# Sliding-window attention and a gated MLP in one kernel: the early heads kept apart by partitions, their copies merged, the planner's constants replaced

## The chip, the core and the metric

The program runs on one NeuronCore of a Trainium2 chip. The metric is the device time of one execution in microseconds (us). TensorE is called PE here, ScalarE ACT, VectorE DVE, GpSimd POOL, and the queue that issues nearly all DMAs is SP. TensorE's clock has two levels, 1.2 and 2.4 GHz; the granted share of the higher one stands in the rows (1.00 is 2.4 GHz).

## What is computed

```python
# q, k, v: (4 batches, 8 heads, 768 positions, 64), float32; n_sink = 4, window = 128
scores = q @ k.transpose(0, 1, 3, 2) / sqrt(64)
keep = (pos_k < n_sink) | ((pos_q - pos_k >= 0) & (pos_q - pos_k < window))
a = softmax(where(keep, scores, -1e9))
x = (a @ v).transpose(0, 2, 1, 3).reshape(3072, 512)
h = x @ w_in              # w_in: 512 x 2048, float64
out = (h * cos(h)) @ w_out  # w_out: 2048 x 512, float64
```

The weights arrive as float64 and are turned into float32 on the chip by integer operations. Products are made either in plain float32 (two records of a matmul in the trace, with two passes over the moving operand each) or in float32r (one pass), with each operand split into a high part and a rest and three float32r matmuls in place of one.

## The kernel before

The 3072 positions are cut into 12 chunks of 256 (`NT`): chunk 0, 1 and 2 are the first 256 positions of the batches 0, 1 and 2, and the others follow. For each chunk the attention of 8 heads gives x transposed (128 partitions for two heads, so four pairs), split into `xhi` and `xlo`; then eight dense slots each compute 256 columns of h (24 matmuls of `h_mm`, line 482), gate them on ACT and DVE, and multiply them into two accumulators of 128 rows (`out_mm`, lines 537 to 542). Chunk 0's `out_mm` runs in plain float32 (line 537), the others in three float32r matmuls (line 542).

The heads of chunks 0 to 2 are the early heads (`NEH` = 24, that is 12 pairs). They see 256 queries and 256 keys, and they stay in plain float32. One pair goes as follows.

- Two DMAs each load q and k of both heads side by side (128 columns, 64 for each head). `pe_turn` (line 887) turns q and then k on PE into the two halves of one PSUM tile `qk` in bank b3.
- `q_out` copies the q half to `tq`. `k_out` copies the k half twice, 64 partitions each, into `kz`: head 0 in partitions 0 to 63 of its first half, head 1 in partitions 64 to 127 of its second half, zeros elsewhere (a memset in `setup`, line 298). These copies are lines 470 on ACT and 472 on DVE, whichever the planner picks.
- `scores_pe` (line 912) makes one matmul for each of the two query blocks j over all 128 partitions; the zeros keep the heads apart. Its moving operand has 2x128 columns for j = 0 and 2x256 for j = 1. Bank "s" holds the scores; in chunk 0, j = 1 uses bank b1.
- `mask` (DVE, line 981), `expo` (ACT, line 990), `denom` and `norm` (lines 1004 to 1015) make the softmax.
- For each head `turn` (line 1087) transposes the three blocks of probabilities, `p_out` copies them to SBUF into the single tile `firsts[:, 0]`, and `values_pe` (line 1139) multiplies them with V. V of both heads is the 128-column stationary operand, so the result of a head has 128 rows of which 64 are of use; the two heads lie side by side in one bank.
- `x_hi` (line 410) is one ACT copy of 64 partitions for each head, `x_minus` (line 417) subtracts it on PE with one 512-column matmul, and `x_lo` is one copy of 64 partitions for each head.

A planner orders all of this before the kernel is written out: every step has a due time made from the constants in `C`, a list of engines with estimated durations, and the steps it waits for. The order on each engine is then fixed, and PE runs its instructions in that order. Until the first matmul of line 537, `fill` (line 1444) puts 256-column dummy matmuls where the plan shows PE idle. The 32 pieces of the weights (512 KB each) are decoded on DVE in three operations each (lines 603, 609, 615) and split on ACT and DVE (lines 642, 645) during the same stretch.

Of the kernel before, what the change touches and what calls it, by code (L numbers as in the profile page):

```python
# [16 lines left out]
P = 128  # L17
# [11 lines left out]
    "AE": 2.711, "ALT": 0.594, "CK": 62.564, "DA": -4.325, "DH": -1.102, "DM": 2.191, "DQ": 2.945, "DS": 4.986,  # L29
    "DV": 3.356, "DX": 0.796, "E": [-3.526, -24.976, 17.898], "GAP": 0.45, "GHI": 2, "GLO": 2, "L": 1, "LAG": 3.882,  # L30
    "LB": 14.146, "LEAD": 15.611, "LP": -23.228, "NE": -17.921, "NEH": 24, "NM": -6.28, "PASS": 2, "PB": 5, "PEN":
    2.331, "PL": 3, "POOLF": 1.446, "POOLPEN": 1.649, "QE": 8.731, "R": 2, "RAW": 3, "S0": -8.701, "S1": 54.633,
    "SE": 2.011, "SO": 5.722, "SO2": -10.441, "STEP": 7.518, "T": 7.132, "TE": [-9.794, -13.102, 9.173], "TQ":
    4.529, "VE": 31.258, "WARM": 4, "WI": -10.037, "WO": 10.858, "WS": 0.701, "WS2": 1.922, "WT": 2, "XE": 5.901,
    "XV": 2,
# [197 lines left out]
def attn_moe_kernel(ctx, tc, q, k, v, n_sink, window, w_in, w_out, out):  # L233
# [56 lines left out]
    def setup():  # L290
# [7 lines left out]
        nc.gpsimd.memset(env.kz, 0.0)  # L298
# [95 lines left out]
    def new_chunk():  # L394
        x = Rec()
        x.acc, x.o, x.f, x.bo = {}, {}, {}, {}
        x.sums = [[] for _ in range(NP)]
        x.parts, x.full, x.om = [], False, {}
        x.last = False
        return x  # L400

    def x_hi(x, a, p, odd):
        def fn(e):
            if p == 0 and not odd:
                x.hi = xp.tile([P, NP, NT], F32R, name=f"xhi_{a}", tag="xhi", bufs=2)
            if odd is None:
                nc.scalar.copy(out=x.hi[:, p, :], in_=x.f[p])
            else:
                r = slice(odd * 64, odd * 64 + 64)
                nc.scalar.copy(out=x.hi[r, p, :], in_=x.f[p][r, odd])  # L410
        return fn

    def x_minus(x, p):
        def fn(e):


            nc.tensor.matmul(
                out=x.f[p], lhsT=minus, rhs=x.hi[:, p, :].unsqueeze(1).broadcast_to([P, 2, NT]),
                start=False, stop=True, skip_group_check=True,
            )  # L420
        return fn

    def x_lo(x, a, p, odd):
        def fn(e):
            if p == 0 and not odd:
                x.lo = xp.tile([P, NP, NT], F32R, name=f"xlo_{a}", tag="xlo", bufs=2)
            if odd is None:
                e.tensor_tensor(out=x.lo[:, p, :], in0=x.f[p], in1=f32(x.hi)[:, p, :], op=ALU.subtract)
            else:
                r = slice(odd * 64, odd * 64 + 64)  # L430
                copy(e, x.lo[r, p, :], x.f[p][r, odd])
        return fn

    def split_x(plan, x, a, p, t, odd=None):

        add, buf = plan.add, plan.buf
        if p == 0 and not odd:
            x.bhi, x.blo = buf("xhi", 2), buf("xlo", 2)
        i = add(
            [("ACT", act(NT, odd is None))], x_hi(x, a, p, odd), x.sums[p] + (x.firsts[:1] if x.parts else [x.bhi]), t, skew=odd == 1  # L440
        )
        if odd == 0:
            x.head, x.first_hi = i, x.parts == []
            if x.first_hi:
                x.firsts, x.parts = [i], [[]]
            else:
                x.parts.append([])
            return [i]
        users = [i]
        if odd is None:  # L450
            j = add(sub(NT), x_lo(x, a, p, odd), [i, x.firsts[1] if x.parts else x.blo], t + 0.3, port=True, lock=True)
            if not x.parts:
                x.firsts = [i, j]
            x.parts.append([i, j])
            return users + [j]
        m = add([("PE", 0.34)], x_minus(x, p), [x.head, i], t + 0.3)
        users.append(m)
        env.minus.users.append(m)
        for half in range(2):
            d = [m] + x.firsts[1:2] if x.firsts[1:] else [m, x.blo]  # L460
            j = add([("ACT", act(NT, False)), ("DVE", dve(NT))], x_lo(x, a, p, half), d, t + 0.6 + 0.01 * half, skew=half == 1)
            if not x.firsts[1:]:
                x.firsts.append(j)
            users.append(j)
        x.parts[p] += [x.head] + users
# [272 lines left out]
    def banded_path():  # L738
# [11 lines left out]
        env.kz = firsts[:, 1].rearrange("p (a n) -> p a n", a=2)  # L750
# [131 lines left out]
        def pe_turn(o, part, tile, n):  # L882
            def fn(e):
                if part == 0:
                    o.qk = ps.tile([P, 2, NT], F32, name=f"qk_{o.tag}", tag="b3")
# [7 lines left out]
        def q_out(o):  # L893
            def fn(e):
                o.tq = ap.tile([P, NT], F32, name=f"tq_{o.tag}", tag="tq")
                copy(e, o.tq, o.qk[:, 0])
            return fn

        def k_out(o, odd):
            def fn(e):  # L900
                r = slice(odd * 64, odd * 64 + 64)
                copy(e, env.kz[r, odd, : o.nkb * P], o.qk[r, 1, : o.nkb * P])
            return fn

        def scores_pe(o, o1, j):
            def fn(e):
                i, w = o.i0 + j, o.w[j]
                pool = env.pa if o.s_banks[j] in ACC else ps
                s_ps = pool.tile([P, 2, NT], F32, name=f"s_{o.tag}_{j}", tag=o.s_banks[j])
                o.s_ps[j], o1.s_ps[j] = s_ps[:, 0], s_ps[:, 1]  # L910
                c0 = max(i - 1 - o.kb0, 0) * P
                nc.tensor.matmul(  # L912
# [754 lines left out]
```

## Time and profile before

| | us |
|---|---|
| median of 3 runs (lowest, highest) | 725.0 (724.86, 725.3) |
| the profiled execution | 725.11 |
| its span, first to last instruction | 723.4 |
| PE, DVE, ACT, POOL busy in it | 711.6, 624.4, 551.7, 104.4 |

Busy time is summed over instructions without overlap. A matmul's end is modelled: it covers the way through the array, so consecutive matmuls overlap in the rows, and what one costs is the step from its start to the next start. A row with "x4" merges four records. The mean granted clock was 0.997.

### The profile page before, as it was taken

The page shows a single profiled execution, that of the slowest core. Times are in us where ns is not written, and L with a number is a line of the kernel's source. Part 1 is how long each engine was busy: PE and PEld are TensorE (multiplying, and loading weights), DVE is VectorE, ACT ScalarE, POOL GpSimd, SP SyncE. Part 2 cuts the span into 40 slices and gives each one's busy share as a digit, 9 for nine tenths or more (in the row PEclk, how much of TensorE's full clock was granted, in tenths as well). Part 3 has the DMA queues.
Part 4 walks back from the last instruction along what each step waited for, and adds up shares of the span by engine and source line. Part 5 has one row for each costly group of instructions (what it writes and reads, how often), then busy time and mean ns, then how long its engine had stood idle before and what let it go on. Part 6 is the DMA issues. An engine that isn't in the chain of part 4 may idle for free.

```text
span 723.4 us, 14936 instructions
## 1 busy us (share of the span) xinstructions
PE 711.6 (98%) x4746; PEld 634.3 (88%) x4746; DVE 624.4 (86%) x1803; ACT 551.7 (76%) x1373; POOL 104.4 (14%) x180
## 2 busy tenths in 40 slices
PE   8999999999999999999999999999999999999996
PEld 6787776999999999999999999999899999999995
DVE  6999999788998999999999999887889998865432
ACT  4989958486978978879879789779788798784431
POOL 1000100002121121121221211322010122212000
PEclk9999999999999999999999999999999999999998
DMA  5886673132852764565465333323232332100001
GB/s 158 225 229 182 209 203 79 34 58 41 208 141 42 175 148 103 140 166 111 109 180 144 83 74 62 71 40 52 49 83 42 68 65 47 33 27 7 31 0 34
DMA packets 215895, 71.47 MB, mean 99 GB/s; under 512 B 204288, under 2 KB 204800, under 8 KB 215808
## 3 DMA queue, kind: packets, MB, share of 16 engines
q1 hardware_dynamic: 215232, 70.17, 40.4%
q8 instruction: 40, 0.66, 0.4%
q14 instruction: 47, 0.39, 0.2%
q10 hardware_dynamic: 576, 0.26, 0.1%
HBM read 64.10 MB, written 6.29 MB: 97 GB/s over the span
## 4 chain that ended last, share of the span: by engine, by line
PE 91%; ACT 4%; DVE 4%; issue 1%; POOL 0%; POOLq 0%; ACTq 0%; DVEq 0%
PE h L482 37%; PE acc L542 33%; PE av L1163 6%; PE s L968 5%; PE acc L537 4%; PE tp L1083 2%; PE av L1139 1%; PE s L912 1%; ACT p L990 1%; PE tp L1087 1%; DVE p L981 1%; ACT firsts L470 1%; PE gp L1067 0%; PE qk L887 0%; DVE p L1015 0%
## 5 line engine op out<-in xcount | busy, mean ns | idle before, releaser
L482 PE MATMUL h<-xhi,lo_in 128*128 128x256 f32 x768 | 226.6, 295 | 0.0
L482 PE MATMUL h<-xlo,hi_in 128*128 128x256 f32 x768 | 217.0, 283 | 0.0
L482 PE MATMUL h<-xhi,hi_in 128*128 128x256 f32 x768 | 216.7, 282 | 0.0
L482 PEld LDWEIGHTS h<-xhi,lo_in 128*128 128x128 f32 x768 | 146.0, 190 | 5.9 <-issue 1.4
L482 PEld LDWEIGHTS h<-xhi,hi_in 128*128 128x128 f32 x768 | 146.2, 190 | 4.4 <-issue 2.1
L482 PEld LDWEIGHTS h<-xlo,hi_in 128*128 128x128 f32 x768 | 146.0, 190 | 0.0
L542 PE MATMUL acc<-hi_out,ghi 128*128 128x512 f32 x350 | 141.4, 404 | 0.0
L542 PE MATMUL acc<-hi_out,glo 128*128 128x512 f32 x350 | 137.4, 393 | 0.0
L542 PE MATMUL acc<-lo_out,ghi 128*128 128x512 f32 x350 | 137.3, 392 | 0.0
L1122 POOL TENSOR_SCALAR_AFFINE_SELECT pz<-pz 128x512 fp32r<-128x512 f32 x128 | 84.8, 662 | 269.6 <-DVE pz L1109 204.5
L990 ACT ACTIVATE p<-p,st 128x264 f32<-128x264 f32 (+1 forms) x192 | 93.2, 488 | 0.3
L491 ACT ACTIVATE yt<-h 128x512 int32<-128x512 f32 x96 | 57.0, 594 | 45.0 <-PE h L482 43.7
L504 ACT ACTIVATE r<-r,neg 128x512 f32<-128x512 f32 x96 | 69.4, 724 | 26.7 <-DVE r L497 26.1
L981 DVE CUSTOM_DVE_ANT_0 p<-s,mk 128x264 f32<-128x264 f32 (+1 forms) x192 | 75.2, 398 | 16.7 <-PE s L968 11.9
L497 DVE SCALAR_TENSOR_TENSOR r<-h,yt 128x512 f32<-128x512 f32 x96 | 65.5, 682 | 23.3 <-ACT yt L491 22.9
L542 PEld LDWEIGHTS acc<-hi_out,glo 128*128 128x128 f32 x350 | 65.8, 188 | 14.8
L509 DVE TENSOR_TENSOR h<-h,r 128x512 f32<-128x512 f32 x88 | 60.8, 691 | 14.3 <-ACT r L504 14.2
L542 PEld LDWEIGHTS acc<-hi_out,ghi 128*128 128x128 f32 x350 | 66.0, 189 | 8.1
L542 PEld LDWEIGHTS acc<-lo_out,ghi 128*128 128x128 f32 x350 | 66.2, 189 | 7.7
L527 DVE TENSOR_TENSOR glo<-h,ghi 128x512 fp32r<-128x512 f32 x88 | 60.1, 684 | 10.4 <-ACT ghi L521 9.9
L521 ACT CAST ghi<-h 128x512 fp32r<-128x512 f32 x88 | 51.5, 585 | 21.0 <-PE acc L542 13.0
L968 PE MATMUL s<-r,l 128*128 128x264 f32 (+2 forms) x288 | 59.6, 288 | 0.0
(139 smaller groups left out, 1262.0 us busy)
## 6 DMA issues: line engine op xcount, KB each, us to landing
raw<-in_moe_w_in_dram SPq DMA_DIRECT2D x32, 512.0 KB
raw<-in_moe_w_out_dram SPq DMA_DIRECT2D x32, 512.0 KB
xk<-in_k_dram SPq DMA_DIRECT2D x256, 48.0 KB
v<-in_v_dram SPq DMA_DIRECT2D x64, 96.0 KB
out_dram<-raw SPq DMA_DIRECT2D x22, 256.0 KB
xq<-in_q_dram SPq DMA_DIRECT2D x144, 32.0 KB
v<-in_v_dram SPq DMA_DIRECT2D x32, 64.0 KB
xq<-in_q_dram SPq DMA_DIRECT2D x24, 64.0 KB
```

The lines of the kernel that those rows point to most:

```text
L482: nc.tensor.matmul(out=o.h[:, t, :], lhsT=w[:, fs], rhs=xx[:, c, :], start=(c == 0 and n == 0), stop=(c == NC - 1 and n == 2),)
L491: nc.scalar.activation(out=yt, in_=o.h, func=AF.Copy, scale=INV2PI, bias=0.25)
L497: nc.vector.scalar_tensor_tensor(out=o.r, in0=o.h, scalar=INV2PI, in1=yt, op0=ALU.mult, op1=ALU.subtract)
L504: nc.scalar.activation(out=o.r, in_=o.r, func=AF.Sin, scale=TWOPI_DOWN, bias=quarter)
L509: nc.vector.tensor_tensor(out=o.h, in0=o.h, in1=o.r, op=ALU.mult)
L521: nc.scalar.copy(out=o.ghi, in_=o.h)
L527: e.tensor_tensor(out=o.glo, in0=o.h, in1=f32(o.ghi), op=ALU.subtract)
L542: nc.tensor.matmul(out=x.acc[j], lhsT=gg[:, t, j * P : (j + 1) * P], rhs=w, start=(f == 0 and n == 0), stop=(f == NFT - 1 and n == 2), ski ...
L968: nc.tensor.matmul(out=o.s_ps[j][:, :w], lhsT=o.l[:, j * P : (j + 1) * P], rhs=r.rearrange("p n s -> p (n s)")[:, c0 : c0 + w], start=(n = ...
L981: nc.vector.tensor_tensor_reduce(out=o.p[:, j, :w], in0=o.s_ps[j][:, :w], in1=masks[min(o.i0 + j, 2)][:, :w], op0=ALU.add, op1=ALU.min, sc ...
L990: nc.scalar.activation(out=o.p[:, j, :w], in_=o.p[:, j, :w], func=AF.Exp, bias=o.lead.st[:, 0, o.nth, j : j + 1], scale=-1.0, accum_out=o. ...
L1122: nc.gpsimd.affine_select(out=env.pz4[:, :, :, n], in_=f32(env.pz4)[:, :, :, 0], pattern=[[0, 2], [0, CB], [sign, P]], compare_op=ALU.is_g ...
```

## The change

For the early heads only:

- q and k are copied together, in one copy of 512 columns, from PSUM to a plain tile `qks`. There is no `kz` with zeros.
- The scores of the two heads are separate matmuls, each on 64 partitions (0 to 63 or 64 to 127 of both operands): four of them in one step, 128 columns each for j = 0 and 256 for j = 1. The first head's scores go to bank "s", the second head's into the bank in which q and k were turned. In chunk 0 that bank alternates between b3 and b1, in chunks 1 and 2 it is b3.
- `p_out` has one buffer for each head of a pair.
- `values_pe` uses the 64 columns of V of its own head and writes to the 64 partitions of that head, so a pair's result is one 128x256 tile.
- `x_hi`, `x_minus` and `x_lo` are done once for a pair, on 128 partitions and 256 columns.
- The planner's constants are other numbers. The later heads and the dense part keep their operations.

```diff
 C = {
-    "AE": 2.711, ... "E": [-3.526, -24.976, 17.898], ... "S1": 54.633, ... "T": 7.132, ...
+    "AE": 17.984, ... "E": [-46.005, -27.161, 3.366], ... "QK": 1, ... "S1": 51.346, ... "T": 8.536, ...
...
-        nc.gpsimd.memset(env.kz, 0.0)
...
-            i = add([("ACT", act(NT, odd is None))], x_hi(x, a, p, odd), ..., skew=odd == 1)
-        m = add([("PE", 0.34)], x_minus(x, p), [x.head, i], t + 0.3)
-        for half in range(2):
-            j = add([("ACT", act(NT, False)), ("DVE", dve(NT))], x_lo(x, a, p, half), d, ...)
+        i = add([("ACT", act(NT, not packed))], x_hi(x, a, p), x.sums[p] + (x.firsts[:1] or [x.bhi]), t)
+            d = [add([("PE", 0.125)], x_minus(x, p), [i], t + 0.3)]
+        on = [("ACT", act(NT, False)), ("DVE", dve(NT))] if packed else sub(NT)
+        j = add(on, x_lo(x, a, p, packed), d + (x.firsts[1:] or [x.blo]), t + 0.6, ...)
...
-                copy(e, o.tq, o.qk[:, 0])
-                copy(e, env.kz[r, odd, : o.nkb * P], o.qk[r, 1, : o.nkb * P])
+                o.qks = ap.tile([P, 2, NT], F32, name=f"qks_{o.tag}", tag="qks", bufs=C["QK"])
+                copy(e, o.qks, o.qk)
...
-                    out=s_ps[:, :, :w], lhsT=o.tq[:, j * P : (j + 1) * P], rhs=env.kz[:, :, c0 : c0 + w],
+                sa = ps.tile([P, 2, NT], F32, name=f"s_{o.tag}", tag="s")
+                for j in range(CB):
+                    c0 = max(o.i0 + j - 1 - o.kb0, 0) * P
+                    for n, (oo, s_ps) in enumerate(((o, sa), (o1, o.qk))):
+                        oo.s_ps[j] = s_ps[:, j]
+                        r = slice(n * D, (n + 1) * D)
+                        nc.tensor.matmul(
+                            out=s_ps[:, j, : o.w[j]], lhsT=o.qks[r, 0, j * P : (j + 1) * P],
+                            rhs=o.qks[r, 1, c0 : c0 + o.w[j]], start=True, stop=True,
+                        )
...
-                o.pt = firsts[:, 0]
+                o.pt = firsts[:, o.odd]
...
-                    x.f[o.pair] = ps.tile([P, 2, NT], F32, name=f"av_{o.tag}", tag=o.av_bank)
+                    x.f[o.pair] = ps.tile([P, NT], F32, name=f"av_{o.tag}", tag=o.av_bank)
+                r = slice(o.odd * D, (o.odd + 1) * D)
-                    dst = x.f[o.pair][:, o.odd, (qs[0] - o.i0) * P : (qs[-1] + 1 - o.i0) * P]
-                    mms.append((dst, o.v2[:, kb - o.kb0], o.pt[:, o.offs[n] * P : o.offs[n + 1] * P]))
+                    dst = x.f[o.pair][r, (qs[0] - o.i0) * P : (qs[-1] + 1 - o.i0) * P]
+                    mms.append((dst, o.v2[:, kb - o.kb0, r], o.pt[:, o.offs[n] * P : o.offs[n + 1] * P]))
...
-            o.s_banks, o.tp_bank, o.av_bank = ("s", "s"), "tp", "av"
+            o.qk_bank, o.tp_bank, o.av_bank = "b3", "tp", "av"
             if o.a == 0:
-                o.s_banks, o.tp_bank, o.av_bank = ("s", "b1"), ("tp", "b4")[o.odd], ("av", "b2")[o.pair % 2]
+                o.qk_bank, o.tp_bank, o.av_bank = ("b3", "b1")[o.pair % 2], ("tp", "b4")[o.odd], ("av", "b2")[o.pair % 2]
...
-                pt, bpt = buf(o.tp_bank, 1), buf("phi", 1)
+                pt, bpt = buf(o.tp_bank, 1), buf(("phi", "plo")[o.odd], 1)
...
+                        o.sc = add([("PE", 4 * 2 * sum(o.w) / 2400)], scores_pe(o, heads[g + 1]), [*o.kr, bs], ...)
+                        o.bqk.users.append(o.sc)
+                        o.bs, heads[g + 1].bs = bs, o.bb
...
-                x.bav.users += split_x(plan, x, o.a, o.pair, t + DA + 5.0, o.odd)
+                if o.odd:
+                    x.bav.users += split_x(plan, x, o.a, o.pair, t + DA + 5.0, True)
```

## Rows read from the trace of the kernel before

**Rows 1.** The page: busy time of each engine and the chain that ended last.

```profile
PE 711.6 (98%) x4746; PEld 634.3 (88%) x4746; DVE 624.4 (86%) x1803; ACT 551.7 (76%) x1373; POOL 104.4 (14%) x180
...
PE 91%; ACT 4%; DVE 4%; issue 1%; POOL 0%; POOLq 0%; ACTq 0%; DVEq 0%
```

**Rows 2.** Windows: length; busy us (records) of PE, PEld, DVE, ACT, POOL; clock; DMA.

```profile
0.00:20.00 20.00, 17.68 (x93) 13.94 (x93) 13.11 (x68) 10.23 (x32) 2.86 (x11) 1.00 0.60 157
20.00:42.75 22.75, 20.33 (x118) 15.55 (x117) 22.36 (x74) 21.87 (x71) 0.00 (x0) 1.00 0.86 233
42.75:57.90 15.15, 15.15 (x111) 13.71 (x110) 14.79 (x40) 12.58 (x31) 0.00 (x0) 1.00 0.69 211
57.90:125.70 67.80, 67.47 (x348) 47.43 (x347) 66.81 (x162) 54.43 (x132) 3.05 (x4) 1.00 0.61 170
```

**Rows 3.** Groups: xcount | busy us, mean ns | idle before; dummies.

```profile
L1444 PE MATMUL idle<-gt 128*128 128x256 f32 x79 | 13.4, 315 | 0.1
```

**Rows 4.** PE in order of time: start, duration, what; idle before, releaser.

```profile
35.75 2.64 PE L1444 MATMUL idle<-gt 128*128 128x256 f32 x20
...
39.29 0.82 PE L1139 MATMUL av<-firsts,v 128*128 128x256 f32 x4
...
41.54 0.92 PE L1139 MATMUL av<-firsts,v 128*128 128x256 f32 x4 [0.98 <-ACT xhi L410]
...
42.75 0.68 PE L482 MATMUL h<-xhi,lo_in 128*128 128x256 f32 x1
...
45.31 0.36 PE L482 MATMUL h<-xhi,lo_in 128*128 128x256 f32 x1
```

**Rows 5.** PE in order of time, steps from start to start.

```profile
43.86 0.39 PE L417 MATMUL av<-xhi,gt 128*128 128x512 f32 x1
44.10 0.49 PE L1087 MATMUL tp<-ident,p 128*128 128x128 f32 x3
...
49.03 0.28 PE L482 MATMUL h<-xhi,hi_in 128*128 128x256 f32 x1
49.15 0.28 PE L482 MATMUL h<-xlo,hi_in 128*128 128x256 f32 x1
...
52.04 1.02 PE L912 MATMUL s<-firsts,tq 128*128 128x512 f32 x2
...
53.13 0.49 PE L1087 MATMUL tp<-ident,p 128*128 128x128 f32 x3
```

**Rows 6.** Windows of line 417 alone: PE and PEld; after the first dense matmul.

```profile
42.75:125.70 82.95, 4.79 (x8) 1.50 (x8) 1.00 0.63 177
125.70:723.40 597.70, 0.75 (x2) 0.19 (x1) 1.00 0.36 81
```

**Rows 7.** Groups again: ACT copies that the change merges, one of 512 columns.

```profile
L491 ACT ACTIVATE yt<-h 128x512 int32<-128x512 f32 x96 | 57.0, 594 | 45.0 <-PE h L482 43.7 <-DVE gc L1053 0.6
...
L410 ACT CAST xhi<-av 64x256 fp32r<-64x256 f32 x24 | 8.8, 366 | 2.7 <-PE av L1139 1.4 <-PE h L482 1.0
...
L470 ACT COPY firsts<-qk 64x256 f32<-64x256 f32 x20 | 7.3, 366 | 5.0 <-PE qk L887 4.6
...
L470 ACT CAST xlo<-av 64x256 fp32r<-64x256 f32 x17 | 6.2, 365 | 0.2
```

**Rows 8.** Windows of line 912 alone (scores), after the first dense matmul.

```profile
42.75:125.70 82.95, 8.96 (x22) 3.02 (x20) 1.00 0.63 177
```

**Rows 9.** PE in time: a later head's values, weights 128 and 64 wide.

```profile
426.26 0.52 PE L1163 MATMUL av<-pz,vr 128*128 128x128 f32 x5
426.62 0.33 PE L482 MATMUL h<-xhi,lo_in 128*128 128x256 f32 x1
426.79 0.28 PE L482 MATMUL h<-xhi,hi_in 128*128 128x256 f32 x1
```

**Rows 10.** PE in order of time, turning of the second pair of chunk 1.

```profile
25.50 0.38 PE L887 MATMUL qk<-ident,xq 128*128 128x128 f32 x2
```

**Rows 11.** DVE in order of time, last mask of the pair turned before it.

```profile
28.94 0.42 DVE L981 CUSTOM_DVE_ANT_0 p<-s,mk 128x256 f32<-128x256 f32 x1
```

## What the change should do to the time

> **What bounds the kernel now.** I read the page first. PE is busy for 98% of the span, and the chain that ended last runs over PE for 91% of it [rows 1]. But busy PE is not useful PE, so the next view is the one by stretches [rows 2]. It shows three regimes. From 0 to 42.75 us PE is not full, though its clock is granted at 1.00 (2.4 GHz) throughout. Its idle time there is (20.00 - 17.68) + (22.75 - 20.33) = 4.7 us, and 79 dummy matmuls stand in that stretch too [rows 3]. At 0.12 us each, the step of a 256-column float32r matmul (49.03 to 49.15) [rows 5], they are 9.5 us. So PE gives away 14.2 us before the first dense matmul at 42.75 [rows 4]. Meanwhile DVE is busy for 22.36 and ACT for 21.87 of the 22.75 us from 20 to 42.75: these two are what ends the head. From 42.75 on PE is full (15.15 of 15.15, then 67.47 of 67.80), with DVE full beside it (66.81 of 67.80) and ACT at 80% [rows 2]. So the time is PE's useful work plus what PE gives away in the head. The change can gain in two ways: less PE work after 42.75, and an earlier end of the head.
>
> The sum goes against the profiled execution: span 723.4 us, 725.11 us with what lies around it, 0.1 above the median of the runs (725.0).
>
> **Part 1, the subtraction on PE.** `x_minus` streams 256 columns in place of 512. Its step now is 43.86 to 44.10, 0.24 us; half of that is 0.12, the step of the dense matmul with as many columns [rows 5]. Of the 12 there are 8 + 2 in the windows after 42.75, one of which lies across the border at 125.7, so 9 [rows 6]. PE saves 9 x 0.12 = 1.1 us on the path. The three before 42.75 shorten only waits.
>
> **Part 2, the copies.** A copy costs by its columns, not by its partitions: the 64-partition copies of q/k halves, `xhi` and `xlo` take 366, 366 and 365 ns, and a 512-column read of PSUM on ACT takes 594 [rows 7]. For each pair:
> - q and k: three copies (3 x 0.366 = 1.10) become one of 0.594. Saved 0.50.
> - `xhi` and `xlo`: two copies each become one of 0.366. Saved 0.37 + 0.37.
>
> By 45.31 us, where the last x of chunk 0 is used [rows 4], eight pairs have been through the first, and chunk 0's four through the second: 8 x 0.50 + 4 x 0.74 = 7.0 us of ACT and DVE time, in a stretch in which both are nearly full [rows 2]. Most of it is ACT's now, but normalizations and copies may go to either, so I halve it: 3.5 us.
>
> A second way to the same number is the tail of the head. The last pair of chunk 0 multiplies V for its even head at 39.29 us; the odd head's matmul waits 0.98 us until 41.54, for the ACT copy `xhi` of the even head, which reads the same bank; and the dense matmuls that need this pair come at 45.31 [rows 4]. After the change there is no copy between the two heads, and the second `firsts` buffer lets the odd head's probabilities be copied ahead. Then: two value products of 0.65 each (three block columns of 128 at two passes for two records, 4 x 384 / 2400 = 0.64), `xhi` 0.37, `x_minus` 0.12 and `xlo` 0.37: 39.29 + 2.16 = 41.45, and 41.85 with an allowance of 0.4 for the four handovers between engines, which is 3.5 us before 45.31. The two readings agree, and I take 3.5. The ends are 0 (DVE's decoding of the weights alone sets the pace, below) and 7.0 (all of the saved time lay on one engine that ends last).
>
> Does it survive to the end? After 57.9 us PE is full, so work that starts earlier ends earlier if DVE follows. DVE is at 66.81 of 67.80 [rows 2], and it gets relief there too: the remaining copies (4 pairs x 0.50 + 8 x 0.74 = 7.9 us over ACT and DVE). ACT, at 80%, can take more of them. So I count the 3.5 in full.
>
> **Part 3, the scores.** The columns streamed per pair stay the same: 2 x 128 + 2 x 256 on 64 rows in place of 256 + 512 on 128. The 512-column matmul now ends with the `x_minus` behind it at 53.13, from 52.04: 1.09 - 0.24 = 0.85 us, so a pair takes 0.85 + 0.43 = 1.28 us [rows 5]. No instruction of this kernel uses part of the array's rows, so the trace can't show if two heads share the array. Upper end: nothing saved. Lower end: each float32 matmul is two records in order, so the second record of one head may run beside the first of the next, with 0.107, 0.107 and 0.213 us of cover: 0.43 per pair. After 42.75 there are 22 records [rows 8], about five pairs of four: 5 x 0.43 = 2.1 us. I take 0, by the scores' own row, and keep 2.1 for a rival.
>
> The Trainium skill speaks for the lower end: "TensorE: Matmul & The Clock Gate", section "Part 3: Packing small matmuls — row/col tiling", says that matmuls on different row groups run at the same time. No run here shows it yet.
>
> **Part 4, the value products.** The 64-column weights change nothing in the columns streamed. Later heads already alternate weights of 128 and 64 columns: five matmuls with 768 columns take 426.26 to 426.62, 0.36 us against 0.32 of pure streaming, and the dense matmul after them steps 0.17 in place of 0.12 [rows 9]. So a change of width costs 0 to 0.05 us, 1 us at most over the 16 heads and 5 score steps after 42.75. I take 0, the nearest to the 0.04 us that the five matmuls themselves lose.
>
> The Trainium skill speaks against the change here: "TensorEngine Tiling (Array Packing)", section "Key Properties", says that changing the tiling mode drains TensorE. By the row above the trace does not agree for columns; for rows it is silent.
>
> **Part 5, the rest.** The zeroing of `kz` is POOL work of the first microseconds, when DVE and PE wait for other things: 0. The DMAs are as many and as large, their order on SP is new. The new constants reorder every queue; after 57.9 us there is nothing left on PE to gain by order (0.33 of 67.80 idle), so they can only move the head, and that is within the ends of part 2.
>
> **A wait is added.** The second head's scores lie in the bank of q and k, so the next turning into that bank waits for this head's masks on DVE. PE runs in order, so everything behind such a turning waits too.
>
> **Sum.** 725.1 - 1.1 - 3.5 + 0 + 0 = 720.5 us.
>
> **The rivals.**
> - *The heads share the array*: the forecast less 2.1, 718.4 us. For it: different partitions, different banks, back to back. Against: no row, and each head's two records stay in order.
> - *DVE's decoding sets the pace*: every dense slot of chunk 0 needs decoded weights, DVE is full from 20 to 125.7 us, and the copies saved are mostly ACT's. Then the head's 3.5 us come back as PE waits between 43 and 125, and only 1.1 us remain: 724.0. The same holds if the reordering eats the gain. Against: copies and normalizations may change engine, and ACT has 13 us to spare in 57.9 to 125.7.
> - *The bank is held* (slower): the second pair of chunk 1 is turned at 25.50 us [rows 10], while the last mask of the pair before it starts at 28.94 and ends at 29.36 [rows 11]. With only bank b3 in chunks 1 and 2 that turning would wait 3.9 us. If two such slips push two pairs' PE work (ten transposes of 128 columns at two passes, 10 x 0.107; scores 1.28; values 1.28; subtraction 0.12: 3.8 us each) past the point where PE has something else, PE loses 7.6 us: 720.5 + 7.6 = 728.1. It decides when both fall into the head, before dense work can fill in; the planner knows of the wait, which speaks against it.
> - *Every change of mode drains PE* (slower): a drain costs what a record lasts beyond its step, 0.28 - 0.12 = 0.16 us [rows 5]. Into and out of the mode for 16 value products and 5 score steps: 42 x 0.16 = 6.7, so 727.2. Against it: the steps of [rows 9]. The page of the Trainium skill named in part 4 states such a drain.
>
> **How the numbers follow.** Chances: forecast 0.38 (its own range 719.5 to 722.5), shared array 0.26, DVE's pace or an eaten gain 0.17, bank 0.14, drain 0.05. A measurement of this kernel can tell about 0.2%, 1.45 us, from no change. Forecast and shared array are faster, 0.64; DVE's pace is the same, 0.17; bank and drain are slower, 0.19. The range runs from 715.5 (the shared array and 3 us more of part 2's upper end) to 726.0 (DVE's pace with 1 us for the changes of width and 1 us of reordering), and leaves out the two slower cases.
>
> **What will show it.** Part 1: `x_minus` records with 256 columns and steps of 0.12. Part 2: fewer dummies than 79, the first dense matmul at about 39 us, no wait of the value products on `xhi`. Part 3: scores of one step that take 1.28 us from first to next (apart) or about 0.85 (shared). Part 4: the dense matmul after value products steps about 0.2. The bank rival: idle PE ahead of the turning, released by DVE's masks. DVE's pace: PE idle on weight pieces between 43 and 125 us. I am wrong if PE is still full from 57.9 on and yet the time grows.

## The result, and the profile after

The changed kernel takes 716.07 us (median of 4 runs, 715.12 to 718.12) against 724.93 (724.86 to 725.3) for the kernel before: a ratio of 0.988 with a 95% interval of 0.9858 to 0.9903, 8.9 us less. The forecast was 720.5. The sign was right and the range held the time, but the gain is nearly twice the 4.6 us of the sum, and it doesn't come from where the sum put it.

The profiled execution of after took 715.12 us, its span is 713.4: 10.0 us under the span of before. The page of after, busy time and the chain that ended last, beside [rows 1]:

```profile
PE 701.1 (98%) x4780; PEld 622.7 (87%) x4780; DVE 615.8 (86%) x1766; ACT 545.1 (76%) x1349; POOL 105.4 (15%) x190
...
PE 93%; DVE 6%; issue 0%; ACT 0%; POOL 0%; POOLq 0%; DVEq 0%
```

Nothing in it has changed its look: PE is still busy for 98% and carries 93% of the chain. The stretches of after, with the columns of [rows 2] (length; busy us and records of PE, PEld, DVE, ACT, POOL; clock; DMA):

```profile
0.00:20.00 20.00, 17.93 (x121) 14.73 (x122) 15.60 (x73) 12.00 (x38) 2.63 (x11) 1.00 0.70 177
20.00:32.75 12.75, 11.24 (x81) 7.85 (x80) 12.72 (x45) 11.61 (x41) 0.00 (x0) 1.00 0.97 260
32.75:42.75 10.00, 9.08 (x72) 7.14 (x72) 9.97 (x34) 7.74 (x22) 0.00 (x0) 1.00 0.85 241
42.75:57.90 15.15, 13.52 (x105) 10.71 (x106) 15.12 (x44) 14.21 (x36) 0.95 (x2) 1.00 0.79 222
57.90:125.70 67.80, 67.58 (x383) 47.23 (x383) 65.55 (x145) 46.05 (x108) 0.93 (x2) 1.00 0.59 165
```

Two columns matter. DVE's: from 20 to 57.9 us it now has 0.09 us free in 37.9. PE's: between 42.75 and 57.9, where it was full before, it is now idle for 1.63 us. The head ends earlier, but PE is not fuller for it. From the order in time on PE, and from its groups (xcount | busy us, mean ns | idle before), the first dense matmul and the dummies of after, to be held against [rows 4] and [rows 3]:

```profile
32.77 0.38 PE L458 MATMUL h<-xhi,lo_in 128*128 128x256 f32 x1
```

```profile
L1411 PE MATMUL idle<-gt 128*128 128x256 f32 x65 | 12.0, 327 | 0.1
```

The first dense matmul starts 10.0 us earlier than at 42.75, yet only 14 of the 79 dummies are gone. If the time were PE's useful work and what PE gives away, a head that ends 10 us earlier would have shown in the second term. It doesn't.

What did shift is the decoding of the weights. Its third operation on `w_out`, the weight whose pieces come last, by line (ns of one: least/middle/most; first and last start us), before and then after:

```profile
L615 DVE SCALAR_TENSOR_TENSOR w_out<-raw,w_out x16: 651/686/696, 44.0 to 114.8; 128x512 int32<-128x512 int32 x16
```

```profile
L591 DVE SCALAR_TENSOR_TENSOR w_out<-raw,w_out x16: 640/684/690, 40.4 to 106.6; 128x512 int32<-128x512 int32 x16
```

The last piece is decoded at 114.8 + 0.69 = 115.5 us before and at 107.3 after: 8.2 of the 10.0 us of span are there at that moment. The stretches on either side of it, before and then after (columns as above):

```profile
20.00:115.49 95.49, 92.75 (x522) 69.72 (x521) 93.91 (x254) 80.34 (x213) 2.34 (x3) 1.00 0.72 203
115.49:723.40 607.91, 601.19 (x4135) 550.68 (x4133) 517.39 (x1483) 461.10 (x1130) 99.19 (x166) 1.00 0.36 81
```

```profile
20.00:107.28 87.28, 82.99 (x532) 59.20 (x532) 87.01 (x233) 71.34 (x189) 1.88 (x4) 1.00 0.78 219
107.28:713.40 606.12, 600.17 (x4130) 548.73 (x4128) 513.23 (x1462) 461.75 (x1124) 100.85 (x175) 1.00 0.36 81
```

PE has 4135 and 4130 records left when the last piece is decoded, and needs 607.9 and 606.1 us for them. With the first 20 us added ([rows 2] before, the window above after), DVE is busy for 107.0 and 102.6 us up to that moment and idle for 8.5 and 4.7. So the 10.0 us are, in bookkeeping: 4.4 less work on DVE before the last decoding, 3.8 fewer DVE waits, 1.8 behind it. The decoding operations are the same 96 in both; the work that went is the copies. DVE's groups up to the last decoding (columns as above), before and then after:

```profile
L472 DVE CAST xlo<-av 64x256 fp32r<-64x256 f32 x5 | 2.1, 423 | 0.1
...
L472 DVE COPY firsts<-qk 64x256 f32<-64x256 f32 x4 | 1.7, 428 | 0.1
L472 DVE COPY tq<-qk 128x256 f32<-128x256 f32 x4 | 1.7, 423 | 4.2 <-PE qk L887 4.1
```

```profile
L448 DVE COPY qks<-qk 128x512 f32<-128x512 f32 x2 | 1.4, 686 | 0.0
...
L448 DVE CAST xlo<-av 128x256 fp32r<-128x256 f32 x1 | 0.4, 415 | 0.0
```

13 copies of 5.5 us have become 3 of 1.8. These are 3.7 of the 4.4 us of work; what is left is a balance of single operations that stand on the other side of the border. Of the waits, the 4.1 us in which DVE sat before a copy of q until PE had turned it are gone. It was a single wait at the very start, from DVE's order in time in before:

```profile
6.64 0.42 DVE L472 COPY tq<-qk 128x256 f32<-128x256 f32 x1 [4.13 <-PE qk L887]
```

In before this copy stands ahead of the building of the masks in DVE's order. In after the first q/k copy is ACT's, and DVE builds the masks from 4.86 us on, after 1.7 us of waiting for a load. The same holds in e6 below (the new operations with the old constants), while e5 (the old operations with the new constants) has a wait of 4.2 us in this place. So this part of the gain comes with the new operations, and by where the first copy stands, not by how long a copy takes.

### The profile page after: what moved, and what is told of

The parts are those of the page before. It is cut to its first block, busy times and chain, and to the rows that moved or that the text cites. A ratio compares the mean times of both kernels' runs of the same rounds, so it can differ in the third digit from the quotient of the medians.

```text
span 713.4 us, 14956 instructions
## 1 busy us (share of the span) xinstructions
PE 701.1 (98%) x4780; PEld 622.7 (87%) x4780; DVE 615.8 (86%) x1766; ACT 545.1 (76%) x1349; POOL 105.4 (15%) x190
## 4 chain that ended last, share of the span: by engine, by line
PE 93%; DVE 6%; issue 0%; ACT 0%; POOL 0%; POOLq 0%; DVEq 0%
PE h L458 38%; PE acc L518 34%; PE av L1132 6%; PE s L938 5%; PE acc L513 4%; PE tp L1053 2%; DVE p L951 1%; PE tp L1057 1%; DVE w_in L585 1%; PE av L1110 1%; DVE w_in L591 1%; PE s L882 1%; PE idle L1411 1%; DVE lo_in L621 1%; PE gp L1037 0%
## 5 line engine op out<-in xcount | busy, mean ns | idle before, releaser
L1092 POOL TENSOR_SCALAR_AFFINE_SELECT pz<-pz 128x512 fp32r<-128x512 f32 x128 | 83.1, 649 | 249.3 <-DVE pz L1079 230.4
L951 DVE CUSTOM_DVE_ANT_0 p<-s,mk 128x264 f32<-128x264 f32 (+2 forms) x168 | 68.1, 405 | 12.6 <-PE s L938 8.9
```

The costliest lines, as they stand in the source:

```text
L951: nc.vector.tensor_tensor_reduce(out=o.p[:, j, :w], in0=o.s_ps[j][:, :w], in1=masks[min(o.i0 + j, 2)][:, :w], op0=ALU.add, op1=ALU.min, sc ...
L1092: nc.gpsimd.affine_select(out=env.pz4[:, :, :, n], in_=f32(env.pz4)[:, :, :, 0], pattern=[[0, 2], [0, CB], [sign, P]], compare_op=ALU.is_g ...
```

## The experiments

Two accounts fit the pair of traces: PE has less to do (scores and value products take fewer us than I allowed for), or DVE is done with the weights sooner. The experiments are made to tell them apart: give each engine work of its own, undo the sharing of the array, undo the copies, exchange the constants. Differences are against after's 716.07 us, of medians; the ratio is against before in the same series.

### Do two heads share the array?

The scores of the pair turned at 37 us, from PE's order in time in after:

```profile
38.37 0.37 PE L882 MATMUL s<-qks 64*128 64x128 f32 x1
38.38 0.37 PE L882 MATMUL qk<-qks 64*128 64x128 f32 x1
38.59 0.27 PE L882 MATMUL s<-qks 64*128 64x128 f32 x1
38.59 0.27 PE L882 MATMUL qk<-qks 64*128 64x128 f32 x1
...
39.23 0.55 PE L1057 MATMUL tp<-ident,p 128*128 128x128 f32 x3
```

The program issues both records of one head, then both of the other; the rows show record beside record, about 10 ns apart, s and qk in turn. The block takes 39.23 - 38.37 = 0.86 us, and all 12 pairs look alike. e1 puts both heads on the same rows:

```diff
-                        r = slice(n * D, (n + 1) * D)
+                        r = slice(0, D)
```

> The changed kernel with the second head's scores made from the first head's 64 rows (so the second head's scores are the first's); order and all else as changed. Theory A, the array is shared and PE's time is what counts everywhere: a pair's four matmuls take about 1.28 us in place of 0.86, 12 pairs x 0.42 = 5.0 us, so about 721.1 us. Theory B, the head (up to the first dense matmul) is set by ACT and DVE and PE's time is free there: only the 5 pairs after it count, 2.1 us, 718.2 us.

Measured: 717.07 us (716.15 to 719.6), ratio 0.9901 (0.9875 to 0.9927): +1.0 us, not apart from after's interval, and less than either theory expected. PE in order of time in e1:

```profile
86.80 0.48 PE L882 MATMUL s<-qks 64*128 64x128 f32 x2
87.13 0.38 PE L882 MATMUL qk<-qks 64*128 64x128 f32 x2
87.35 0.59 PE L882 MATMUL s<-qks 64*128 64x256 f32 x2
87.78 0.59 PE L882 MATMUL qk<-qks 64*128 64x256 f32 x2
88.31 0.55 PE L1057 MATMUL tp<-ident,p 128*128 128x128 f32 x3
```

Here the heads go one after the other, 88.31 - 86.80 = 1.51 us. So different rows are what lets them run together, and it saves 0.65 us for a pair, 7.8 for the 12. But giving these 7.8 us back (by the steps; PE's busy time rises by 5.6 us, from 701.1 to 706.7) costs about 1.0 us of time.

The value products do the same by columns, which no step of the prediction had foreseen. Of a pair in after (eight records, then the next dense matmul and its successor):

```profile
63.55 0.88 PE L1110 MATMUL av<-firsts,v 128*64 128x256 f32 x8
64.36 0.39 PE L458 MATMUL h<-xhi,lo_in 128*128 128x256 f32 x1
64.58 0.28 PE L458 MATMUL h<-xhi,hi_in 128*128 128x256 f32 x1
```

That is 0.81 us where two heads in turn were worked out at 1.28. e2 takes V of both heads as the weights again, 128 columns into 128 partitions, so that the second head writes over the first and the first head's values are left out:

```diff
-                    dst = x.f[o.pair][r, (qs[0] - o.i0) * P : (qs[-1] + 1 - o.i0) * P]
-                    mms.append((dst, o.v2[:, kb - o.kb0, r], o.pt[:, o.offs[n] * P : o.offs[n + 1] * P]))
+                    dst = x.f[o.pair][:, (qs[0] - o.i0) * P : (qs[-1] + 1 - o.i0) * P]
+                    mms.append((dst, o.v2[:, kb - o.kb0], o.pt[:, o.offs[n] * P : o.offs[n + 1] * P]))
```

> The changed kernel with each head's value products on the whole array again: 128 columns of V, 128 rows of the pair's tile, the second head writing over the first (so the first head's values are lost). Theory A: the two heads can't run side by side, 10 pairs that stand next to each other take 1.3 in place of 0.81 us, +4.9 us, about 721 us. Theory B: only the pairs after the first dense matmul count, 8 x 0.49 = 3.9 us, about 720 us. If the values never shared the array: no change, 716 us.

Measured: 716.41 us (715.84 to 717.5), ratio 0.9878 (0.9861 to 0.9894): +0.3 us, no difference. PE in order of time in e2:

```profile
100.01 1.47 PE L1110 MATMUL av<-firsts,v 128*128 128x256 f32 x8
101.23 0.36 PE L458 MATMUL h<-xhi,lo_in 128*128 128x256 f32 x1
```

1.22 us instead of 0.81, and again the time takes no notice; both theories that priced the sharing expected 720 us or more. e3 makes both edits at once.

> Both edits of the two runs before at once: scores of both heads on the same 64 rows, values on the whole array. Theory A: the two add up, about 716.1 + 5.0 + 4.9 = 726 us, so that nothing of the gain over the kernel before (724.9) is left to the merged copies. Theory B: 716.1 + 2.1 + 3.9 = 722 us, some 3 us of the gain is the copies'.

Measured: 719.35 us (718.98 to 719.71), ratio 0.9919 (0.9902 to 0.9936): +3.3 us, for some 12 x 0.65 + 10 x 0.41 = 11.9 us of PE work (of 10 pairs the value products stand side by side in after). Up to the last decoding PE is idle for 2.9 us in e3 and for 6.4 in after: the added work goes first where PE waits. By PE's busy time the addition is 7.7 us (701.1 to 708.8), so a quarter to under a half of it shows. This is less than either theory expected (722 and 726). PE is not what sets the time in this stretch, or not alone.

### Which engine sets the pace?

e8d issues two needless DVE copies of 128x512 in SBUF behind each of the 12 q/k copies, e8a one such copy on ACT. The planner doesn't know of them, so the order stays. The tile `spare` is set to zero once at the start, on POOL (not shown).

```diff
                 copy(e, o.qks, o.qk)
+                for _ in range(2):                            # e8d
+                    nc.vector.tensor_copy(out=spare, in_=spare)
```

```diff
                 copy(e, o.qks, o.qk)
+                nc.scalar.copy(out=spare, in_=spare)          # e8a
```

> The changed kernel with two more copies of 512 columns, SBUF onto itself, on DVE behind each of the 12 copies of q and k; nothing waits for them but DVE's own queue. At 0.4 us each that is 9 to 10 us of DVE. If DVE sets the pace until the weights are decoded (about 105 us): 8 to 10 us slower, 724 to 726. If PE or ACT does: within 2 us of 716.

> The same with one copy of 512 columns on ACT behind each of the 12 copies of q and k, about 0.6 us each, 7 us of ACT. If DVE alone sets the pace: within 2 us of 716. If ACT stands in the same chain (the split copies cost 11.6 us and lay mostly on ACT): 4 to 7 us slower, 720 to 723.

Measured: e8d 724.13 us (722.05 to 725.4, 10 runs), ratio 0.9984 (0.997 to 0.9999), +8.1 us; e8a 716.15 us (714.51 to 716.84), ratio 0.9878 (0.9852 to 0.9904), +0.1 us. The groups of e8d and of e8a:

```profile
L875 DVE COPY spare<-spare 128x512 f32<-128x512 f32 x24 | 10.2, 423 | 0.4
```

```profile
L874 ACT COPY spare<-spare 128x512 f32<-128x512 f32 x12 | 7.6, 630 | 0.0
```

Two DVE copies in a row take 0.80 us from the first to the next operation, for example in e8d:

```profile
28.74 0.88 DVE L875 COPY spare<-spare 128x512 f32<-128x512 f32 x2
29.54 0.42 DVE L581 TENSOR_SCALAR w_in<-raw 128x512 int32<-128x512 int32 x1
```

So DVE got 12 x 0.80 = 9.6 us more, as its busy time up to the last decoding says too (112.2 against 102.6), and the kernel became 8.1 us slower: nearly one for one. ACT's copies step at 0.52 us, 6.2 us in all, which cost nothing. In e8d the last decoding, by line, and the stretches around its end:

```profile
L593 DVE SCALAR_TENSOR_TENSOR w_out<-raw,w_out x16: 640/682/690, 46.1 to 115.4; 128x512 int32<-128x512 int32 x16
```

```profile
0.00:116.08 116.08, 102.37 (x651) 74.21 (x652) 112.19 (x329) 84.35 (x226) 4.97 (x16) 0.99 0.69 195
116.08:722.90 606.82, 600.21 (x4130) 548.63 (x4128) 513.39 (x1462) 461.95 (x1124) 101.20 (x175) 1.00 0.36 80
```

The last piece is decoded 8.8 us later than in after, PE has the same 4130 records left then, and takes the same time for them (606.8 and 606.1 us). PE's idle time up to that point rose from 6.4 to 13.7 us. This shows that DVE's work sets the pace of the changed kernel up to the last decoding. The same split over all kernels run:

| kernel | last piece decoded, us | DVE idle till then | span | span from then on |
|---|---|---|---|---|
| before | 115.5 | 8.5 | 723.4 | 607.9 |
| after | 107.3 | 4.7 | 713.4 | 606.1 |
| e1 scores on the same rows | 109.3 | 5.9 | 714.4 | 605.1 |
| e2 values whole | 108.8 | 5.8 | 715.8 | 607.0 |
| e3 both | 109.9 | 6.5 | 718.0 | 608.1 |
| e8d more DVE | 116.1 | 3.9 | 722.9 | 606.8 |
| e8a more ACT | 108.8 | 5.3 | 714.9 | 606.1 |
| e4 all copies split | 117.1 | 11.3 | 723.4 | 606.3 |
| e4q q/k copies split | 111.3 | 6.8 | 717.6 | 606.3 |
| e4x x copies split | 111.9 | 7.8 | 719.0 | 607.1 |
| e5 before, new constants | 117.1 | 9.7 | 725.1 | 608.0 |
| e6 after, old constants | 110.9 | 5.6 | 720.7 | 609.8 |
| e10 copies on ACT only | 111.5 | 5.7 | 718.2 | 606.7 |
| e11 normalization off DVE too | 110.2 | 6.0 | 718.2 | 608.0 |

The last column varies by 4.7 us, the first by 9.8. It is an association and no law: e6 loses 3.7 us more behind the border than after does, and why was not found. Each row is a single execution, and those of e2, e3, e6 and e10 were the slowest of their four (e6's by 2.0 us over its median).

### What are the merged copies worth?

e4 keeps the changed kernel and splits the copies again as before had them: three for q and k, two of 64 partitions each for `xhi` and `xlo`, in the same order and on the same engines. e4q splits q and k alone, e4x `xhi` and `xlo` alone.

```diff
-                copy(e, o.qks, o.qk)                          # e4, e4q
+                copy(e, o.qks[:, 0], o.qk[:, 0])
+                for n in range(2):
+                    r = slice(n * D, (n + 1) * D)
+                    copy(e, o.qks[r, 1], o.qk[r, 1])
...
-            nc.scalar.copy(out=x.hi[:, p, :], in_=x.f[p])     # e4, e4x
+            if x.packed:                                      # the early heads
+                for n in range(2):
+                    r = slice(n * 64, n * 64 + 64)
+                    nc.scalar.copy(out=x.hi[r, p, :], in_=x.f[p][r])
+            else:
+                nc.scalar.copy(out=x.hi[:, p, :], in_=x.f[p])
...
-                copy(e, x.lo[:, p, :], x.f[p])                # e4, e4x
+                for n in range(2):
+                    r = slice(n * 64, n * 64 + 64)
+                    copy(e, x.lo[r, p, :], x.f[p][r])
```

> The changed kernel with its copies cut as before: q and k in three copies, xhi and xlo in two of 64 partitions each, on the same engine and in the same order. That puts 12 x 1.2 = 15 us back on ACT and DVE, some 7 us of it before the first dense matmul. Theory A (PE's work alone is the gain): within 1 us of 716. Theory B, as forecast: 3.5 us slower, 719.6; up to 7 where the copying engine is the one that ends last, 723.

> The changed kernel with the copy of q and k alone cut in three again, same engine and order. 12 x 0.5 = 6 us more, 10 of the 12 on ACT. The 7.6 us that were put on ACT behind these copies cost nothing, so time on ACT as such is free. If what counts is that the scores, and then DVE's masks, wait longer for the copy (DVE runs in order): the larger part of the 11.6 us of the split copies, 6 to 9 us, 722 to 725. If only DVE's own time counts (2 of the 12 copies): 1 us, 717.

> The changed kernel with xhi and xlo alone cut in two again, same engine and order. 12 x 0.74 = 9 us more, nearly all on ACT. If the split copies cost by the wait of DVE behind the scores: small, 1 to 3 us, 717 to 719, since no mask waits for xhi or xlo. If they cost by ACT's time in the order: 7 us, 723.

Measured: e4 727.71 us (725.11 to 729.1, 10 runs), ratio 1.0043 (1.0028 to 1.0057), +11.6 us, slower than before itself. e4q 719.03 us (718.57 to 719.99), ratio 0.9919 (0.9897 to 0.994), +3.0; e4x 720.57 us (718.03 to 722.67), ratio 0.9934 (0.9913 to 0.9956), +4.5. So in after's order the gain hangs on the copies, on both kinds of them: with all of them split nothing of it is left, while e3, without both sharings and with the merged copies, keeps 5.6 of the 8.9 us. But this order was made for merged copies, so the 11.6 us are their price in it and not what they bring by themselves; e5 below, all the old operations under the new constants, is as slow (727.41). All three missed their expectations: e4 is slower than either theory allowed (723 at most), e4q lies between its two (717, and 722 to 725), and e4x, in which no mask waits for `xhi` or `xlo`, lost more than the 1 to 3 us of the way over the masks and less than the 7 of ACT's time.

How e4's DVE waits between 20 and 105 us (waiting line, releaser: us in total, times, longest; the first three), and then PE's up to the last decoding (two of them):

```profile
DVE p L962 <- PE s L893: 1.7, 1, 1.7
DVE p L962 <- ACT p L994: 1.1, 1, 1.1
DVE r L481 <- ACT yt L475: 1.0, 1, 1.0
```

```profile
PE av L415 <- ACT xhi L408: 3.2, 4, 1.2
PE s L893 <- ACT qks L454: 2.3, 5, 0.9
```

In after, no DVE wait stands in that stretch at all. PE waits for ACT's copies, the masks on DVE wait for PE's scores, and DVE runs in order, so the decoding behind the masks waits with them: DVE's idle time is 11.3 us against 4.7 (the other 3.1 us by which its last decoding is late are busy time). This would also explain how e8a and e4 go together: ACT's busy time is free, the length of the way from turning over copy and scores to the mask is not. e4x shows a second way: PE waits 3.6 us in three waits for `xhi` there, and what stands behind in PE's order, scores among it, comes later. Both ways were read from the waits; no run isolates either of them.

The two halves don't add up in the medians: 3.0 + 4.5 = 7.5 of 11.6. In the profiled spans they do: 4.2 + 5.6 = 9.8 of 10.0, but e4's profiled execution was the fastest of its ten. TensorE's granted clock fell for a while in this execution. In e4's windows (columns as above) it stands at 1.00 up to 22 us, and at 0.50 (1.2 GHz) from 24 to 26, after PE had been busy for only 1.29 and 1.38 us of two stretches of 2:

```profile
20.00:22.00 2.00, 1.29 (x11) 1.05 (x10) 1.76 (x11) 1.92 (x7) 0.00 (x0) 1.00 1.10 246
22.00:24.00 2.00, 1.38 (x9) 1.08 (x9) 1.66 (x4) 1.94 (x7) 0.00 (x0) 0.88 0.86 272
24.00:26.00 2.00, 2.00 (x10) 1.02 (x9) 0.97 (x4) 1.97 (x9) 0.00 (x0) 0.50 1.01 221
```

What made it fall is not shown: in e4x PE was busy for only 0.13 us of the two from 24 to 26, and the clock stayed at 1.00. Its share in e4's 11.6 us was not separated, but the means of the runs speak for a small one: e4's two runs with a mean clock of 0.997, as in the profiled executions of before, e4q and e4x, took 727.14 and 727.62 us, and its three at 0.990 took 728.47 to 728.82. e8d has a dip too (0.99 up to the last decoding); its four runs with a mean of 0.997 or more took 722.05 to 724.36 us, so most of its 8.1 us is there without one.

### Operations or constants?

e5 is the kernel before with the new constants, e6 the changed kernel with the old ones (and one buffer for `qks`):

```diff
-    "AE": 2.711, "ALT": 0.594, "CK": 62.564, ... "S1": 54.633, ... "T": 7.132, ...
+    "AE": 17.984, "ALT": 0.863, "CK": 42.675, ... "S1": 51.346, ... "T": 8.536, ...
```

> The kernel before with the planner's new constants alone. Theory O (the operations bring the gain, the constants only fit them): no faster than before, 724 to 730 us. Theory K (the new order brings it, by starting the decoding of the weights 3.6 us earlier): about 720 us.

> The changed kernel with the planner's old constants (and QK = 1, which the old ones lack). Theory O: most of the gain stays, 716 to 719 us. Theory K: 721 us or more.

Measured: e5 727.41 us (725.91 to 728.85, 9 runs), ratio 1.0037 (1.0024 to 1.005), 2.5 us slower than before; e6 720.55 us (720.23 to 722.53), ratio 0.9944 (0.9922 to 0.9966), 4.4 us faster than before's 724.93. Both together bring 8.9. So the constants are worth 4.5 us on the new operations and cost 2.5 on the old ones: they are fitted to the operations, not good in themselves. e5 came out as theory O has it; e6 lies between the two theories (716 to 719, and 721 or more).

### Can more be taken from DVE?

If DVE sets the pace, work should leave it. e10 lets the early q/k, `p_out` and `xlo` copies go to ACT only, e11 does that and keeps the early normalizations to POOL and ACT:

```diff
-    [("ACT", act(2 * NT, False)), ("DVE", dve(2 * NT))], qk_out(o), ...
+    [("ACT", act(2 * NT, False))], qk_out(o), ...
...
-    [("POOL", ...), ("DVE", ...), ("ACT", ...)], norm(o, j), ...
+    [("POOL", ...), ("ACT", ...)] if o.early else [("POOL", ...), ("DVE", ...), ("ACT", ...)], norm(o, j), ...     # e11
```

> The changed kernel with the early heads' copies (q and k, probabilities, xlo) given to ACT alone, so that the planner can't put any on DVE. It takes 8 copies, 4.4 us, from DVE. If DVE's own time sets the pace until the weights are decoded, and the new order is as good: 4 us faster, 712. If the order that the planner finds loses as much: 716, or slower.

> The same, and the early heads' normalizations on ACT or POOL alone: another 21 operations, 5.0 us, from DVE. By DVE's own time: 9 us faster than the changed kernel, 707. By ACT as the next bound (5 us of normalizations become 8 us there, each some 0.4 us, with the exponentials behind them): 712 to 718.

Measured: e10 718.73 us (717.15 to 719.89), ratio 0.9906 (0.9881 to 0.9932), +2.7; e11 719.98 us (719.51 to 720.37), ratio 0.9931 (0.991 to 0.9951), +3.9. Both lost. DVE's busy time up to the last decoding did not fall (105.8 and 104.2 us, after 102.6): the planner made a new order in which DVE does other work ahead of the decoding (9 and 12 splits of `w_out` and 8 operations on `vs`, where after has 4 and none). e11 is slower than both of its expectations. So these two runs speak on the planner and not on the theory. Whether a plan that keeps after's order with fewer copies on DVE would gain was not tried. None of the kernels run beats after.

## Why the prediction came right, and which of its terms did not

**What bounds the kernel.** This step failed. I read "PE is full from 42.75 on" [rows 2] as "the time is PE's useful work and what it gives away in the head", and put DVE, full in the same rows (66.81 of 67.80), beside it as a rival with 0.17. With two engines full, the rows can't say which one the other follows. The added work says it for the changed kernel: 7.8 us on PE cost 1.0 (e1) and 11.9 cost 3.3 (e3), while 9.6 us on DVE cost 8.1 (e8d). The account by PE would even have fitted the pair of traces afterwards; only the experiments rule it out as the whole.

**DVE's pace, the rival.** The right engine with the wrong price. I let the gain shrink to 1.1 us, because "the copies saved are mostly ACT's". What it missed: DVE got rid of 10 copies before the last decoding itself, 3.7 us, and of its one long wait, the 4.1 us before the first copy of q. That its waits for scores and exponentials can hang on the copies on ACT shows in e4 (DVE idle 11.3 us against 4.7); in before they were short (1.1 us for scores, 0.2 for exponentials). The sign that I named for it, PE idle on weight pieces, is hardly there. Who waits for the third decoding operation in after (us, times):

```profile
  ACT hi_out L618: 6.6, 6
...
  PEld acc L513: 0.2, 1
```

The planner fixed PE's order with estimated durations of DVE's steps, so I take it that the pace shows as dummies and as idle time ahead of other steps rather than as a wait for a piece; no run tests that.

**Part 1, the subtraction.** Forecast 0.12 us a step, 1.1 us in all. In after, PE in order of time, the subtraction and the matmul behind it:

```profile
46.85 0.38 PE L410 MATMUL av<-xhi,gt 128*128 128x256 f32 x1
47.08 0.28 PE L458 MATMUL h<-xhi,lo_in 128*128 128x256 f32 x1
```

That is 0.23 us, and 0.20 at 51.40, against 0.24 before. The 0.12 is the step within a row of like matmuls; one that stands alone among others costs more. So 0.01 to 0.04 us a step were saved in place of 0.12, at most 0.4 us for the nine: mis-sized, and on an engine that doesn't set the time here.

**Part 2, the copies.** Forecast 3.5 us, ends 0 and 7.0. In after's order the result hangs on this part, and there it was too small: splitting them again costs 11.6 us (e4), 3.0 for q and k alone and 4.5 for `xhi` and `xlo` alone. Reading the gain as an earlier head was the wrong move (the two readings that agreed on 3.5). The head's end moved by 10.0 us, from 42.75 to 32.77, where about 39 was forecast, and it doesn't carry the gain: e4's first dense matmul starts at 37.61, 5.1 us earlier than before's, and e4 is no faster than before. Two signs of this part came true: 65 dummies, and in after no wait of the value products on `xhi`.

**Part 3, the scores.** I took 0 and kept 2.1 us for sharing in part. The heads share more than that: 0.86 us for a pair, and 1.51 when both heads stand on the same rows. That my mark for "shared" was 0.85 is chance, since it came from one record running beside the next, with nothing for going in and out. The argument against it, that each head's two records stay in order, is refuted by the rows of 38.37 us. As a mechanism the rival was right, and it is worth 1.0 us of time, within the noise (e1).

The Trainium skill says in "TensorE: Matmul & The Clock Gate", section "Part 3: Packing small matmuls — row/col tiling", that matmuls on different row groups run at the same time; the trace agrees, with the 0.86 against 1.51 us.

**Part 4, the value products.** Forecast 0, for a change of width alone. The dense matmul behind them steps 64.58 - 64.36 = 0.22 us, as said. That two heads share the array by columns as well (0.81 against 1.22 us) was missed; it changes the time by 0.3 us, no difference (e2). Both sharings together are worth 3.3 us (e3), where the two runs add up to 1.3; the intervals are too wide to say that they matter more together.

**The drain, the rival at 727.2.** Wrong as a slowdown, but there is a cost, and it is not much smaller than the rival's 0.32 us for going in and out. It shows best where a head's value products stand alone, in after and then in e2 with the whole array:

```profile
74.62 0.86 PE L1110 MATMUL av<-firsts,v 128*64 128x256 f32 x4
75.41 1.98 PE L513 MATMUL acc<-w_out,g 128*128 128x512 f32 x4
```

```profile
75.32 0.82 PE L1110 MATMUL av<-firsts,v 128*128 128x256 f32 x4
75.97 1.88 PE L513 MATMUL acc<-w_out,g 128*128 128x512 f32 x4
```

The block takes 0.79 us in place of 0.65, and it starts 0.21 us after the dense matmul ahead of it in place of 0.12: 0.23 us in all. A pair that stands together pays this once (0.81 us for both heads), and the sharing gives back more. The scores fit: 0.86 us a pair, where each head streams two records of 384 columns with two passes each, 0.64 us at 2.4 GHz. The Trainium skill states that a change of the tiling mode drains TensorE ("TensorEngine Tiling (Array Packing)", section "Key Properties"); the trace agrees that something is paid, these 0.23 us. In the later heads [rows 9] the change of width costs 0.04 and 0.05 us; why the two differ was not found.

**Part 5, the constants.** Forecast 0, "they can only move the head". They are worth 4.5 us on the new operations (e6 against after). The step that failed is the first one again: a reordering that gets DVE to the last decoding earlier (at 107.3 us in place of e6's 110.9) moves everything behind it. That e6's 4.4 us come near the sum's 4.6 is chance, since the sum had the terms elsewhere. So is it that the range held the time, by 0.6 us: its lower end (718.4 less 3, which is 715.4) was made of a sharing that brought about 1 us and of an earlier head.

**The wait that was added.** It is there and small. PE's waits in after, of the turning for the masks:

```profile
PE qk L862 <- DVE st L951: 1.6, 2, 0.9
```

Twice, 1.6 us in all, where the rival had two slips of 3.8. It stands on PE, which has idle time in that stretch.

## What to carry to other kernels

Where two engines are full in the same rows, busy shares and the chain don't tell which one sets the time: put a few needless operations on each in turn and see what they cost (here 8.1 of 9.6 us on DVE, 0.1 of 6.2 on ACT). Then look for the last instruction of the slow engine that the rest depends on, and compare kernels by when it ends and by what is left behind it. Price a saved copy by the chain in which it stands, not by its engine's busy time, and count a planner's constants as part of the operations they were fitted to.

## What the runs showed of the hardware that I had not expected

Float32 matmuls of two heads on different 64 rows run record beside record, about 10 ns apart, although the program has both records of one head before the other's: 0.86 us for a pair against 1.51 on the same rows. Value products of two heads that use different 64 columns of the array share it too: 0.81 against 1.22 us. One head alone on 64 columns is not cheaper than the pair (0.79 us), and dearer than on the whole array (0.65 us). And TensorE's granted clock fell to 1.2 GHz from 24 to 26 us in e4, after PE had been idle for 1.3 us of 4; in e4x it stayed at 2.4 GHz although PE was idle for 1.87 us of 2, so the rows give no rule for it.
